# Pooled attention and a gated conv FFN on one core: the last output tile's halves in PSUM tiles of their own, and a new order of all queues

## The chip, the core and the metric

The kernel runs on one core of a Trainium2 chip. The metric is the device time in microseconds of one execution. TensorE (PE in the profile) does matmuls, VectorE (DVE) and ScalarE (ACT) elementwise work, GpSimd (POOL) and SyncE (SP) issue DMAs here, SyncE also the crossbar transposes.

## What is computed

With B = 8 batches, 8 heads, 576 rows and head size 64, in float32 outside and bfloat16 inside:

```python
k_p = k.reshape(B, H, Sp, 8, D).mean(axis=3)        # Sp = 72
v_p = v.reshape(B, H, Sp, 8, D).mean(axis=3)
attn = softmax(q @ k_p.T / sqrt(D))                  # 576 x 72 a head
x = (attn @ v_p), heads side by side                 # B, 576, 512
h = relu(x @ w_in)                                   # 512 -> 1024
gate = sigmoid(depthwise conv of h over 3 rows)
out = (h * gate) @ w_out                             # 1024 -> 512, float32
```

## The kernel before

All work is written down as some 1,075 small steps by a planner (`pl.add`), each with its engine, what it reads and writes, and the PSUM slot that it takes (`take`) or frees (`give`). In which order the steps are issued is not worked out in the kernel: it is the string `order` in `PARAMS`, a list of step numbers. Each engine and each DMA queue runs its steps in that order, waiting where a step needs another's result. The string also gives a matmul step its PSUM slot (`@A0` to `@A2` of twice 512 columns, `@B0` and `@B1` of 512), and `106A0/77` puts 106 units of filler matmuls (128 columns each, L231) ahead of step 77. The string `act` names the steps that ScalarE does out of those that VectorE could do as well. The table `alt` picks a variant of a step: for `x3.0`, 1 means a crossbar transpose issued by SyncE, none means four transposes on TensorE and a copy out of PSUM.

The names of the steps, with b the batch, t a tile of 128 rows, f one of 8 slices of the 1024 columns:

- `kT`, `kz`: the pooled k turned, and copied out of PSUM (L501, L507). `cw`: the conv weights in place (L361); `dw`: the identity scaled by one of them, for convs on TensorE (L407, L409).
- `qT`, `qTe`: q of batch 0 turned and copied (L567, L573); `qg`, `qD`: q of a later batch regrouped (L261) and turned by two crossbar transposes (L608).
- `sc`, `exp`: scores on TensorE and their exponential on ScalarE (L625 to L652). `av`, `rc`, `nm`: attention times v (L670, L674), reciprocal of the sums (L683), and the division (L687).
- `xt`, `xte` or `xD`: the tile of x turned, by TensorE and a copy (L701, L705) or by the crossbar (L710).
- `mm1`, `relu`: x times w_in (L732 for batch 0, L747) and relu (L738, L753).
- `cp`, `ca`, `conv`: the conv, as products and sums on ScalarE and VectorE (L769 to L781) or as matmuls (L800); `tanh`, `tg1`, `g`: the gate and its product with h, into `gT` (L788, L832, L838).
- `mm2`, `oe`, `st`: gT times w_out (L860), the copy out of PSUM (L883, or L873 for the last tile's halves), the store (L887, L878).

Two batches make a pair of nine output tiles; `mm2.3.8` is the last tile of the last pair. In the last pair, tiles 4 to 8 are summed in two pieces, slices 0 to 5 and then 6 and 7 (`cuts`). Of tile 8, the first piece is 512 columns wide, the second piece two halves of 256 columns in the same PSUM tile; each half is copied and stored by itself.

Of the kernel before, what the change touches and what calls it, by code (L numbers as in the profile page):

```python
# [56 lines left out]
    ),  # L57
    "act": (
# [7 lines left out]
    ),  # L66
    "alt": {"q1": 1, "v1": 1, "c0.5": 2, "c0.7": 2, "q2": 1, "c1.1": 1, "c1.3": 2, "q3": 1, "x3.0": 1, "x3.1": 1, "x3.2": 1, "x3.3": 1, "x3.4": 1, "c2.1": 1, "c2.5": 1, "q4": 1, "x4.0": 1, "x4.1": 1, "x4.2": 1, "x4.3": 1, "x4.4": 1, "c3.5": 1, "q5": 1, "x5.0": 1, "x5.1": 1, "x5.2": 1, "x5.3": 1, "x5.4": 1, "q6": 2, "x6.0": 1, "x6.1": 1, "x6.2": 1, "x6.3": 1, "x6.4": 1, "q7": 2, "x7.0": 1, "x7.1": 1, "x7.2": 1, "x7.3": 1, "x7.4": 1},
    "nq": 2,
    "nr": 1,
    "nx": 4,  # L70
# [72 lines left out]
def kernel(  # L143
# [10 lines left out]
    nc = tc.nc  # L154
# [3 lines left out]
    P = 128  # L158
# [809 lines left out]
```

## Time and profile before

| | us |
|---|---|
| median of 3 runs | 198.35 |
| lowest, highest | 197.63, 200.87 |
| the profiled execution | 196.67 |
| its span, first to last instruction | 195.0 |
| TensorE, VectorE, ScalarE, GpSimd busy | 186.5, 166.1, 167.0, 46.7 |
| TensorE clock granted | 1.00 all through |

The profiled execution is one of its own and a little faster than the three timed ones; its time is its span and 1.67 us around it. In the rows, `x4` is a count, and `<-` behind an idle time names what ended it. Two engines' rows that overlap in time ran beside each other. Matmuls overlap by a pipeline, so for them the distance of two starts tells the cost, not the length of one row.

### The profile page before, as it was taken

What the parts mean: (1) busy time and instruction counts of PE and PEld (TensorE: products, weight loads), DVE (VectorE), ACT (ScalarE), POOL (GpSimd) and SP (SyncE); (2) the same over time, 40 slices, a digit from 0 to 9 for tenths busy, and PEclk for the clock granted to TensorE, in tenths of its full rate; (3) what the DMA queues carried; (4) which work ended last, traced back from release to release, by engine and by line L of the source; (5) the groups of instructions that cost most, each with busy time, mean ns of one, the idle gap of its engine ahead of it and who ended that gap; (6) DMA issues with size and microseconds to landing.
All of it is one profiled execution on the core that took longest, in us unless ns stands there. A gap on an engine that the chain in (4) does not pass through costs nothing.

```text
span 195.0 us, 4515 instructions
## 1 busy us (share of the span) xinstructions
PE 186.5 (96%) x1730; PEld 124.3 (64%) x1746; DVE 166.1 (85%) x388; ACT 167.0 (86%) x301; POOL 46.7 (24%) x85
## 2 busy tenths in 40 slices
PE   7997999989999999999999999999999999999992
PEld 2465977665788878667667766685666566654441
DVE  3757789998589999999999899999999898999620
ACT  2088999955379999999999999999999999999931
POOL 8993354272055004363035000000000000000000
PEclk9999999999999999999999999999999999999999
DMA  5999999999939999999789999394003464105444
GB/s 193 210 163 202 203 203 208 203 206 204 152 50 172 203 205 157 195 96 201 152 135 180 200 296 140 89 186 118 14 0 95 151 196 170 54 0 217 170 156 161
DMA packets 40746, 30.72 MB, mean 158 GB/s; under 512 B 18556, under 2 KB 35668, under 8 KB 40724
## 3 DMA queue, kind: packets, MB, share of 16 engines
q0 software_dynamic: 17920, 15.67, 52.0%
q1 hardware_dynamic: 22804, 14.76, 30.2%
q8 instruction: 13, 0.21, 0.4%
q14 instruction: 9, 0.07, 0.1%
HBM read 32.52 MB, written 9.44 MB: 215 GB/s over the span
## 4 chain that ended last, share of the span: by engine, by line
PE 56%; ACT 17%; DVE 15%; DMA 8%; issue 2%; ACTq 0%; DVEq 0%
PE psfB L860 23%; PE psfA L747 17%; DMA q_b<-in_q_dram 5%; PE psfA L670 3%; ACT tg L788 3%; DMA osb<-in_k_dram 3%; ACT hT L753 3%; DVE gT L838 2%; DVE cv L776 2%; PE psfA L860 2%; DVE cv L781 2%; ACT cv L769 2%; DVE tg L832 2%; PE psfA L800 2%; PE psfA L674 2%
## 5 line engine op out<-in xcount | busy, mean ns | idle before, releaser
L860 PE MATMUL psfB<-w_out,gT 128*128 128x512 bf16 x260 | 62.2, 377 | 1.1 <-issue 0.3
L747 PE MATMUL psfA<-xT,w_in 128*128 128x288 bf16 x448 | 60.6, 286 | 0.0
L747 PEld LDWEIGHTS <-w_in 128*128 128x128 bf16 x448 | 43.3, 98 | 12.7 <-issue 0.2
L860 PEld LDWEIGHTS <-gT 128*128 128x128 bf16 x290 | 27.7, 98 | 30.4 <-issue 1.6
L788 ACT ACTIVATE tg<-cv,cs 128x576 bf16<-128x576 bf16 x54 | 42.2, 830 | 0.4 <-DVE cv L781 0.3
L753 ACT ACTIVATE hT<-psfA 128x576 bf16<-128x576 f32 x56 | 37.5, 692 | 4.8 <-PE psfA L747 4.5
L769 ACT ACTIVATE cv<-hT,cr 128x576 bf16<-128x576 bf16 x38 | 29.9, 830 | 0.0
L687 DVE TENSOR_TENSOR xx<-psfA,rr 128x512 bf16<-128x512 f32 x40 | 26.9, 687 | 0.7
L771 DVE TENSOR_SCALAR cv<-hT,cr 128x576 bf16<-128x576 bf16 x70 | 24.0, 369 | 1.1 <-ACT hT L738 0.7
L838 DVE TENSOR_TENSOR gT<-tg,hT 128x1152 bf16<-128x1152 bf16 x32 | 23.9, 754 | 0.4
L883 ACT COPY osb<-psfB 128x512 f32<-128x512 f32 x33 | 20.5, 643 | 4.2 <-PE psfB L860 3.0
L652 ACT ACTIVATE attnT<-psfA 128x576 bf16<-128x576 f32 x35 | 21.9, 664 | 0.5 <-PE psfA L644 0.3
L781 DVE TENSOR_TENSOR cv<-cv 128x1152 bf16<-128x1152 bf16 (+1 forms) x29 | 20.4, 710 | 1.1 <-ACT cv L769 0.5
L776 DVE TENSOR_TENSOR cv<-cv,hT 128x1152 bf16<-128x1152 bf16 (+1 forms) x29 | 20.5, 708 | 0.3 <-ACT cv L769 0.2
L295 POOL DMA_DIRECT2D v_b<-in_v_dram x32 | 16.3, 518 | 14.8 <-DVE vs L533 7.0
L670 PE MATMUL psfA<-vblk,attnT 128*128 128x130 bf16 x160 | 15.6, 221 | 1.3 <-ACT attnT L633 0.9
L832 DVE TENSOR_SCALAR tg<-tg 128x1152 bf16<-128x1152 bf16 x32 | 14.3, 454 | 1.6 <-ACT tg L788 1.5
L670 PEld LDWEIGHTS <-attnT 128*128 128x128 bf16 x160 | 11.8, 98 | 4.2 <-ACT attnT L633 1.3
L683 DVE RECIPROCAL rr<-psfA 128x8 f32<-128x8 f32 x40 | 7.3, 194 | 5.8 <-PE psfA L674 5.7
L231 PE MATMUL pswA<-zero 128*128 128x512 bf16 (+1 forms) x43 | 10.3, 385 | 1.1 <-DVE zero L333 1.1
L674 PE MATMUL psfA<-vblk,attnT 128*128 128x130 bf16 x80 | 11.2, 221 | 0.0
L644 PE MATMUL psfA<-qT,kz 128*128 128x288 bf16 x56 | 10.2, 286 | 0.1
(107 smaller groups left out, 220.4 us busy)
## 6 DMA issues: line engine op xcount, KB each, us to landing
out_dram<-osb SPq DMA_DIRECT2D x14, 512.0 KB, 3.7
q_b<-in_q_dram POOLq DMA_DIRECT2D x7, 576.0 KB, 9.4
k_b<-in_k_dram POOLq DMA_DIRECT2D x7, 512.0 KB, 10.0
v_b<-in_v_dram POOLq DMA_DIRECT2D x7, 512.0 KB, 8.4
out_dram<-osb SPq DMA_DIRECT2D x7, 256.0 KB, 2.2
osb<-in_k_dram SPq DMA_DIRECT2D x1, 1024.0 KB, 5.2
w_in<-in_moe_w_in_dram POOLq DMA_DIRECT2D x2, 512.0 KB, 10.1
w_out<-in_moe_w_out_dram POOLq DMA_DIRECT2D x2, 512.0 KB, 11.4
```

What stands on the lines that cost most here:

```text
L652: nc.scalar.activation(out=at(m)[:, t, :].rearrange("p (r i j) -> p r i j", i=2, j=3), in_=slot(key)[:, :, 0:HC].rearrange("p i (j r) -> p ...
L670: nc.tensor.matmul(out=a[:, g, c * w:(c + 2) * w], lhsT=attnT[m][:, S * s + u0:S * s + u0 + P], rhs=vblk[m][:, 2 * s:2 * s + 2, :].rearran ...
L687: nc.vector.tensor_tensor(out=xx[i3].rearrange("p (g h e) -> p g h e", g=2, h=4), in0=av_view()[:, :, :, 0:D], in1=rr[i3].rearrange("p (g ...
L747: nc.tensor.matmul(out=t[:, i, 0:HC], lhsT=w_in[:, c, f * P:(f + 1) * P], rhs=xT[m][:, c, i * HC:(i + 1) * HC], start=(c == 0), stop=(c == ...
L753: nc.scalar.activation(out=hT[m][:, f, 2:S + 2].rearrange("p (i x) -> p i x", i=2), in_=slot(key)[:, :, 0:HC], func=ACT.Relu)
L769: nc.scalar.activation(out=cv[y][:, kk // 2, z, :], in_=src, func=ACT.Copy, scale=sc)
L771: nc.vector.tensor_scalar(out=cv[y][:, kk // 2, z, :], in0=src, scalar1=sc, scalar2=None, op0=OP.mult)
L776: nc.vector.tensor_tensor(out=cv[y][:, 0, 0:n, :], in0=cv[y][:, 0, 0:n, :], in1=H4[:, f:f + n, 2:S + 2], op=OP.add)
L781: nc.vector.tensor_tensor(out=cv[y][:, 0, 0:n, :], in0=cv[y][:, 0, 0:n, :], in1=cv[y][:, 1, 0:n, :], op=OP.add)
L788: nc.scalar.activation(out=tg[i3][:, z, :], in_=cv[y][:, 0, z, :], func=ACT.Tanh if half else ACT.Sigmoid, scale=cs[:, f + z:f + z + 1] if ...
L838: nc.vector.tensor_tensor(out=o_, in0=tg[i3], in1=hT[b % 2][:, f:f + 2, 2:S + 2], op=OP.mult)
L860: nc.tensor.matmul(out=a[:, 0, j0:j1], lhsT=g[:, c, t * P:(t + 1) * P], rhs=w_out[:, c, j0:j1], start=(c == 0), stop=(c == n_fb - 1), skip ...
```

## The change

Three things change. First, each half of the last tile is a matmul group of its own over all eight slices, in a PSUM tile of its own, and each copy frees its own tile:

```diff
-                parts = [(0, 512)] if not final or c1 < n_fb else [(0, 256), (256, 512)]
+                parts = [(0, 256), (256, 512)] if final else [(0, 512)]
                 for y, (j0, j1) in enumerate(parts):
+                    key = (kind, pair, t, y) if final else (kind, pair, t)
+                    ky = ok + (y,) if final else ok
...
-                            nc.tensor.matmul(out=a[:, 0, j0:j1], lhsT=g[:, c, t * P:(t + 1) * P],
-                                             rhs=w_out[:, c, j0:j1], start=(c == 0), stop=(c == n_fb - 1), skip_group_check=final)
+                            nc.tensor.matmul(out=a[:, 0, 0:j1 - j0], lhsT=g[:, c, t * P:(t + 1) * P],
+                                             rhs=w_out[:, c, j0:j1], start=(c == 0), stop=(c == n_fb - 1))
...
                 for y in range(2):
+                    key = (kind, pair, t, y)
...
-                        copy_on(e)(out=osb[i3][:, 0, y * 256:(y + 1) * 256], in_=slot(key)[:, 0, y * 256:(y + 1) * 256])
+                        copy_on(e)(out=osb[i3][:, 0, y * 256:(y + 1) * 256], in_=slot(key)[:, 0, 0:256])
...
-                                reads=[ok + (y,)], writes=[("osb", i3, y)], give=key if y else None, after=oi)
+                                reads=[ok + (y,)], writes=[("osb", i3, y)], give=key, after=oi)
```

Second, `alt` loses `"x3.0": 1`, so that one piece of x is turned by TensorE. Third, the strings `order` and `act` are others: nearly every step moves on its engine, 71 steps change between ScalarE and VectorE, and the fillers are 180 units where they were 163 (106 of them ahead of the first `kT` in both). One line of the old and new string:

```diff
-        "15 52 0 41 4 44 16 53 47 18 49 60 50 57 61 46 56 58 73 55 3 17 74 59 75 54 76 5 43 1 106A0/77@B0 48 6@B1 86 78 7 51 28 19 29 "
+        "15 52 0 41 4 47 18 53 49 19 48 61 50 60 57 3 59 5 16 73 56 54 74 58 55 75 76 65 106A0/77@B0 6@B1 84@A0 7 36 21 78 86 17 85 62 42 "
```

Lines behind L854 stand three to five lines later in the changed kernel (L860 is L863, L873 is L878, L887 is L892).

ScalarE at the start, before and then changed. `dw` is the scaled identity, `kz` and `qT` the turned k and q of batch 0, `attnT` the exponentials; the words in brackets name the engine whose count a row waits for.

```order
L507 ACT_TABLE_LOAD [waits DVE_49]
L507 COPY kz_85<-psbB 64x4x72 [waits PE_49]
L407 ACTIVATE dw_114<-ident,cw 128x128 [waits DVE_49,Pool_49]
L407 ACTIVATE dw_115<-ident,cw 128x128
L341 COPY wrm<-wrm 128x1
L507 COPY kz_85<-psbB 64x4x72
L573 COPY qT_87<-psbB 128x12x64 [waits PE_49]
L573 COPY qT_87<-psbA 128x12x64 [waits PE_49]
L573 COPY qT_87<-psbB 128x24x32 [waits PE_49]
L633 ACTIVATE attnT_89<-psfB 128x384 [waits PE_49]
```

```order
L407 ACT_TABLE_LOAD [waits DVE_49]
L407 ACTIVATE dw_117<-ident,cw 128x128 [waits Pool_49]
L573 COPY qT_87<-psbA 128x24x32 [waits PE_49]
L573 COPY qT_87<-psbB 128x12x64 [waits PE_49]
L507 COPY kz_85<-psbB 64x4x72 [waits DVE_49]
L573 COPY qT_87<-psbA 128x12x64 [waits PE_49]
L633 ACTIVATE attnT_89<-psfB 128x384 [waits PE_49] x2
L633 ACTIVATE attnT_89<-psfA 128x384 [waits PE_49]
L407 ACTIVATE dw_116<-ident,cw 128x128
L633 ACTIVATE attnT_89<-psfB 128x384 [waits PE_49]
```

The table load is put ahead of ScalarE's first instruction and takes over its wait for VectorE: before, that was for the zeroing of kz, VectorE's second instruction; now it is for cw, its twelfth. One of the two kz copies has gone to VectorE, and the other stands between the qT copies.

VectorE around the second regrouping copy of q for batch 7 (`q_80<-q_b_79`), before and then changed. `rr` and `xx` are the reciprocal and the division of batch 6's attention tiles, `tg` and `gT` batch 3's gate, `cv` batch 4's conv.

```order
L447 TENSOR_TENSOR k_b_75<-k_b_75 128x5x128
L838 TENSOR_TENSOR gT_110<-tg_106,hT_102 128x2x576
L838 TENSOR_TENSOR gT_110<-tg_108,hT_102 128x2x576
L683 RECIPROCAL rr_94<-psfA 128x8
L683 RECIPROCAL rr_93<-psfA 128x8
L261 COPY q_80<-q_b_79 96x6x256
L771 TENSOR_SCALAR cv_104<-hT_101,cr 128x576
L687 TENSOR_TENSOR xx_97<-psfA,rr_93 128x512
```

```order
L687 TENSOR_TENSOR xx_98<-psfA,rr_94 128x512
L776 TENSOR_TENSOR cv_105<-cv_105,hT_101 128x1152
L683 RECIPROCAL rr_91<-psfA 128x8
L771 TENSOR_SCALAR cv_103<-hT_101,cr 128x576
L687 TENSOR_TENSOR xx_95<-psfA,rr_91 128x512
L261 COPY q_80<-q_b_79 96x6x256
L683 RECIPROCAL rr_92<-psfA 128x8
```

The copy stood ahead of the division of batch 6's first tile; now it stands behind that of its third. SyncE's two crossbar transposes for the scores of batch 7 follow it.

ScalarE at the end, the copies of the last output tiles, before and then changed (with the tiles' numbers).

```order
L883 COPY osb_111<-psfB_2896 128x512
L883 COPY osb_111<-psfB_2905 128x512
L883 COPY osb_111<-psfA_2918 128x512
L873 COPY osb_111<-psfB_2933 128x256 x2
L963 UNCONDITIONAL_BRANCH
```

```order
L888 COPY osb_111<-psfB_2907 128x512
L888 COPY osb_111<-psfA_2924 128x512
L878 COPY osb_111<-psfB_2936 128x256
L878 COPY osb_111<-psfB_2945 128x256
L968 UNCONDITIONAL_BRANCH
```

Both halves were read from one PSUM tile; now each is read from its own. On TensorE the first half's eight matmuls of 256 columns come first and the second half's eight after them, as the last work of that engine.

More of the change, by code (lines that the diff above doesn't have):

```diff
@@ L16 @@
     "order": (
[40 rows of a table removed]
[40 rows of a table added]
     ),
     "act": (
[7 rows of a table removed]
[7 rows of a table added]
     ),
-    "alt": {"q1": 1, "v1": 1, "c0.5": 2, "c0.7": 2, "q2": 1, "c1.1": 1, "c1.3": 2, "q3": 1, "x3.0": 1, "x3.1": 1, "x3.2": 1, "x3.3": 1, "x3.4": 1, "c2.1": 1, "c2.5": 1, "q4": 1, "x4.0": 1, "x4.1": 1, "x4.2": 1, "x4.3": 1, "x4.4": 1, "c3.5": 1, "q5": 1, "x5.0": 1, "x5.1": 1, "x5.2": 1, "x5.3": 1, "x5.4": 1, "q6": 2, "x6.0": 1, "x6.1": 1, "x6.2": 1, "x6.3": 1, "x6.4": 1, "q7": 2, "x7.0": 1, "x7.1": 1, "x7.2": 1, "x7.3": 1, "x7.4": 1},
+    "alt": {"q1": 1, "v1": 1, "c0.5": 2, "c0.7": 2, "q2": 1, "c1.1": 1, "c1.3": 2, "q3": 1, "x3.1": 1, "x3.2": 1, "x3.3": 1, "x3.4": 1, "c2.1": 1, "c2.5": 1, "q4": 1, "x4.0": 1, "x4.1": 1, "x4.2": 1, "x4.3": 1, "x4.4": 1, "c3.5": 1, "q5": 1, "x5.0": 1, "x5.1": 1, "x5.2": 1, "x5.3": 1, "x5.4": 1, "q6": 2, "x6.0": 1, "x6.1": 1, "x6.2": 1, "x6.3": 1, "x6.4": 1, "q7": 2, "x7.0": 1, "x7.1": 1, "x7.2": 1, "x7.3": 1, "x7.4": 1},
     "nq": 2,
@@ L859, in fn @@
                         for c in range(c0, c1):
-                            nc.tensor.matmul(out=a[:, 0, j0:j1], lhsT=g[:, c, t * P:(t + 1) * P],
-                                             rhs=w_out[:, c, j0:j1], start=(c == 0), stop=(c == n_fb - 1), skip_group_check=final)
-                    i = pl.add(f"mm2.{pair}.{t}.{c0}" + (f".{y}" if len(parts) > 1 else ""), "PE", (0.2165 * (j1 - j0) / 512 + 0.002) * (c1 - c0), fn,
+                            nc.tensor.matmul(out=a[:, 0, 0:j1 - j0], lhsT=g[:, c, t * P:(t + 1) * P],
+                                             rhs=w_out[:, c, j0:j1], start=(c == 0), stop=(c == n_fb - 1))
+                    i = pl.add(f"mm2.{pair}.{t}.{c0}" + (f".{y}" if final else ""), "PE", (0.2165 * (j1 - j0) / 512 + 0.002) * (c1 - c0), fn,
                                reads=[("gT", pair % 2, c, z) for c in range(c0, c1) for z in halves] + [("wo", 0), ("wo", 1)]
-                               + ([ok] if c0 else []),
-                               writes=[ok + (y,)] if len(parts) > 1 else [ok], take=key,
+                               + ([ky] if c0 else []),
+                               writes=[ky], take=key,
                                after=last_o[0] if not c0 else None)
```

92 rows, old and new, of the table PARAMS are left out of this document.

## The prediction

> **What bounds the kernel now.** I read the page's head first, then a table by stages, then the chain of waits backward from the end.
>
> ```profile
> span 195.0 us, 4515 instructions
> PE 186.5 (96%) x1730; PEld 124.3 (64%) x1746; DVE 166.1 (85%) x388; ACT 167.0 (86%) x301; POOL 46.7 (24%) x85
> ```
>
> ```profile
> core 0: us, PE busy (x) PEld busy (x) DVE busy (x) ACT busy (x) POOL busy (x), PEclk, DMA share, GB/s
> 15.00:30.00 15.00, 13.94 (x190) 11.42 (x191) 11.47 (x39) 14.08 (x38) 6.96 (x12) 1.00 1.25 203
> 30.00:42.70 12.70, 11.84 (x159) 8.89 (x159) 12.47 (x28) 10.79 (x23) 5.75 (x10) 1.00 1.24 205
> 42.70:75.00 32.30, 32.17 (x413) 24.06 (x415) 27.99 (x66) 24.16 (x43) 7.75 (x12) 1.00 1.09 169
> 75.00:125.00 50.00, 49.35 (x398) 34.01 (x402) 48.23 (x112) 49.19 (x84) 12.69 (x22) 1.00 1.00 168
> 125.00:165.00 40.00, 39.67 (x289) 25.86 (x293) 38.32 (x85) 39.68 (x67) 0.00 (x0) 1.00 0.44 118
> 165.00:191.40 26.40, 26.24 (x139) 13.43 (x139) 19.41 (x39) 22.17 (x38) 0.00 (x0) 1.00 0.31 121
> ```
>
> The reader is to see that from 42.7 to 191.4 us TensorE idles 0.13 + 0.65 + 0.33 + 0.16 = 1.27 us in 148.7. Busy could hide waits, so I looked at how fast it streams, in the chain of waits.
>
> ```profile
> 164.34 3.92 PE psfA L747 x32
> 173.67 6.20 PE psfB L860 x28
> 191.35 0.03 ACTq L873
> 191.42 0.37 ACT osb L873
> 191.79 0.27 ACTq L963
> ```
>
> 32 matmuls of 288 columns take 0.1225 us each and 28 of 512 columns 0.221 us, back to back. So from 42.7 us **TensorE's own work is the bound**: a new order there gains at most the 1.27 us, while each wait that it makes on TensorE is paid in full. VectorE and ScalarE are nearly as full (48.23 and 49.19 of 50 us in the third stage), so such waits are easily made. From 30.0 to 42.7 us VectorE is the full one (12.47 of 12.70), from 15 to 30 us ScalarE (14.08 of 15). After 191.4 us comes the tail.
>
> **The change part by part.** The sum is made against the profiled execution: 196.67 us, its span of 195.0 and 1.67 around it. The median of the runs shown is 198.35, 1.68 above that, and I add 1.68 at the end.
>
> *The tail.* Here are the last rows of ScalarE and SyncE on the timeline, and what the two stores' line says of landing.
>
> ```profile
> 191.42 0.65 ACT L873 COPY osb<-psfB 128x256 f32<-128x256 f32 x2 [1.07 <-PE psfB L860]
> 191.82 0.81 SPq L878 DMA_DIRECT2D out_dram<-osb  x2
> DMA to landing us min/median/max: 1.7/1.7/1.7
> ```
>
> Both copies start only after the last matmul, the second 0.28 after the first (0.65 less 0.37); the second store is issued at 191.82 + 0.81 - 0.38 = 192.25 and lands 1.7 us later, in the last us of the span. In the changed kernel the first half is complete 8 matmuls of 256 columns (half of 0.221, so 0.88 us) before the end; its copy (0.37) and store issue (0.33) lie beside those matmuls. The second half's copy then starts where the first one's did, and its store at 191.82 instead of 192.25: **-0.43 us**. On TensorE, six 512-column matmuls become twelve of 256, the same columns; I take 0 for it. Bounds: 0 if the store before it still holds up the queue, -0.65 if both copies went. For TensorE nothing is late behind it: it is its last work.
>
> *The transposed piece x3.0.* It leaves SyncE's crossbar transposes for TensorE.
>
> ```profile
> 42.23 0.39 PE L701 MATMUL psbB<-ident,xx 128*128 128x128 bf16 x4
> 42.45 0.22 PE L231 MATMUL pswB<-zero 128*128 128x128 bf16 x1
> L710 SPq DMA_TRANSPOSE xT<-xx x25: 1171/1230/2393, 72.3 to 156.6; - x25
> ```
>
> Four transposes take 42.45 - 42.23 = **+0.22 us** of TensorE, which is full there. The SyncE issue that goes (1.23 us) was not on the chain: I give no gain for it. The new copy out of PSUM goes to ScalarE.
>
> ```profile
> L771 DVE TENSOR_SCALAR cv<-hT,cr 128x576 bf16<-128x576 bf16 x70 | 24.0, 369 | 1.1 <-ACT hT L738 0.7 <-ACT tg L788 0.5
> L705 DVE COPY xT<-psbB 128x512 bf16<-128x512 bf16 x4 | 1.7, 415 | 0.3 <-PE psbB L701 0.3
> ```
>
> Between ScalarE and VectorE, by the order, 23 conv products leave ScalarE and 18 come; one kz copy and one output copy more leave than come; five copies of xT more come, x3.0's among them. VectorE gets five products at 24.0/70 = 0.34 us and the kz and output copies, and loses four xT copies at 0.42: about 1 us more, an estimate. This costs nothing as long as TensorE has work queued, and is kept in the upper bound below.
>
> *The start.* ScalarE and its partners before the first real work:
>
> ```profile
> 1.39 1.28 ACT L507 ACT_TABLE_LOAD   x1 [1.39 <-DVE kz L414]
> 9.42 0.39 ACT L507 COPY kz<-psbB 64x288 bf16<-64x288 bf16 x1 [6.74 <-PE psbB L501]
> 9.91 0.69 ACT L407 ACTIVATE dw<-ident,cw 128x128 bf16<-128x128 bf16 x2
> 11.55 0.80 ACT L573 COPY qT<-psbB 128x768 bf16<-128x768 bf16 x1 [0.46 <-PE psbB L567]
> 12.25 0.80 ACT L573 COPY qT<-psbA 128x768 bf16<-128x768 bf16 x1
> 13.65 0.50 ACT L633 ACTIVATE attnT<-psfB 128x384 bf16<-128x384 f32 x1
> 9.63 0.18 DVE L361 TENSOR_SCALAR cw<-psfB 128x24 f32<-128x24 f32 x1
> 16.23 0.40 PE L670 MATMUL psfA<-vblk,attnT 128*128 128x130 bf16 x4 [0.94 <-ACT attnT L633]
> ```
>
> Before, the table load sat at 1.39, hidden in ScalarE's idle 9 us. In the new order its first instruction is a scaling of the identity by cw, and the table load in front of it waits for VectorE up to cw, which ends at 9.81. Load 9.9 to 11.2; scaling, about 0.3; then from 11.5 three qT copies at 0.70 apart and one kz copy (0.4) in between end at about 14.1 (the last takes 0.8). The fill of 35 in front of the first score matmul ends there too: the qT transposes end about 12.25 and 35 x 0.0533 (a 512-column filler takes 0.213) is 1.87. So the first score starts near 14.15, the first exp near 14.55 against 13.65, and the first attention-times-v matmul near 14.55 + (16.23 - 13.65) = 17.1: **0.9 us late**.
>
> It does not stay. The first output product, at 42.72, waits for the last gate product, and for that VectorE is the bound:
>
> ```profile
> 23.49 0.82 DVE L443 TENSOR_TENSOR k_b<-k_b 128x1280 bf16<-128x1280 bf16 x1
> 26.45 0.70 DVE L771 TENSOR_SCALAR cv<-hT,cr 128x576 bf16<-128x576 bf16 x1 [0.67 <-ACT hT L738]
> 41.74 0.75 DVE L838 TENSOR_TENSOR gT<-tg,hT 128x1152 bf16<-128x1152 bf16 x1
> 42.72 2.53 PE L860 MATMUL psfB<-w_out,gT 128*128 128x512 bf16 x11
> ```
>
> From the row at 23.49 to the one at 41.74 both orders hold 45 VectorE instructions, and differ in six small ones on each side. With the lag of 0.9 the row at 23.49 would still start near 23.5, because in the new order the constants that stood ahead of it come elsewhere. The conv product at 26.45 had waited 0.67 for ScalarE; its slice came out of relu as first and seventh; the slice now taken first comes as second and fourth, so I give 0.2 of the 0.67 back: **-0.2 us** at 42.72. Bounds: -0.67, and +0.9 if VectorE cannot make up the lag. The fills after 16 us shrink from 29 units to 22, which is in this.
>
> A rule of the Trainium skill speaks against this part: the page "ScalarE: Activation LUTs", section "What ACT_TABLE_LOAD costs", gives a table load 1283 ns and a drain of about 1380 ns with it. The load agrees with the 1.28 us row; no drain shows behind it here, since ScalarE had nothing to do until 9.42. By that rule the start would be another 1.38 us later.
>
> *The last head's transpose, q of batch 7.* VectorE's regrouping copy now stands behind the row at 129.28 instead of at 122.44.
>
> ```profile
> 122.44 0.51 DVE L261 COPY q<-q_b 96x1536 bf16<-96x1536 bf16 x1
> 129.28 0.69 DVE L687 TENSOR_TENSOR xx<-psfA,rr 128x512 bf16<-128x512 f32 x1
> 125.13 3.01 SPq L608 DMA_TRANSPOSE qT<-q  x2
> DMA to landing us min/median/max: 3.5/3.8/4.6
> 133.17 0.65 PE L644 MATMUL psfA<-qT,kz 128*128 128x288 bf16 x4
> ```
>
> The two crossbar transposes start 3.01/2 = 1.5 apart, and the last lands up to 4.6 after its start: 6.1 from the first issue. The scores that need them stood at 133.17; by the order one output product (8 x 0.217 = 1.73) and x3.0 now stand ahead, so TensorE comes there at 135.1. VectorE reaches the copy between 128.3 (four conv instructions, 1.9 us, have gone behind it, others in front) and 129.97; it ends at 128.9 to 130.5 and the landing is at 135.0 to 136.6. TensorE waits 0 to 1.5, and every matmul behind it with it. I take **+0.2**, near the lower end, as the 1.9 us that left weigh more than what came.
>
> *All other places.* Some hundred instructions change places on full engines. The trace of before shows what that can give back, 1.27 us, and what it can cost only by its nearest rows: VectorE's extra 1 us, and single waits like the 0.94 at 16.23. I take 0, bounds -1.3 and +2.
>
> Sum: -0.43 + 0.22 - 0.2 + 0.2 + 0 = -0.2. So 196.5 us for a profiled execution and 196.5 + 1.68, about **198.1 us**, for a median. A measurement of this kernel can tell about 2%, some 4 us, from no change.
>
> **The rivals.** *The table load comes through.* If VectorE makes up nothing of the 0.9, the sum ends at +0.9 instead of -0.2 there: 199.2 us, slower than before. For it: the row at 41.74 shows VectorE full up to the end of that stage, so it has no slack to catch up with. Against: the lag ends before VectorE's full stretch starts at 26.45. It decides from the point where the first relu results come later than VectorE's k sums are done.
>
> *ScalarE is not free right behind its table load.* In the rows of before nothing stands on it from 2.67 to 9.42, so they do not exclude it. One more stretch of the load's own length, 1.28, on top of the lag gives 200.5 us. Against: nothing in the rows shows such a stretch. The page named above has this drain, and with its 1.38 it would be 200.6.
>
> *A landing in the middle.* The q transposes land at the late end, 136.6, and another such wait joins it at a piece of xT: +1.5 and +1 over the forecast's +0.2, 200.4 us. More than 2% slower would need almost 4 us of waits on TensorE; three times the worst that I find.
>
> *The waits go.* The 1.27 us of idle after 42.7 vanish, as do the 0.86 before (12.70 - 11.84): 198.1 - 2.1 = 196.0 us. For it: they are scattered, so a finer order can take them. Against: full engines make new ones. Faster by 2% would need a further 2 us, only to be had from the start, which I see later, not earlier.
>
> *The tail does not shorten.* If the halves' copies stay together, for instance since the stores queue behind the one before, 0.43 is lost: 198.5 us.
>
> **How the numbers follow.** Forecast, within a us of 198.1: 0.56, of which the rival of the tail has 0.06. The lag comes through: 0.10. ScalarE busy behind the load: 0.05. A landing: 0.09. Waits go: 0.20. From these, slower by over 2% is 0.04 (parts of the second to fourth), faster by over 2% 0.04 (the far end of the last), and 0.92 lies within. The range reaches from waits gone (196.0, less 0.3, part of the start's lower bound) to the landing with the tail's 0.43 lost as well (200.8): 195.7 to 200.8. Single runs shown lie between 197.63 and 200.87, which asks for no less.
>
> **What would show it.** Right: ScalarE's table load at about 9.9 us; the first output product within 0.7 of 42.7; one L701 group of four more; the copy of the first half about 0.8 us ahead of the last matmul's end, and about 3.2 us from that end to the end of the span (195.0 - 191.35 = 3.65 before). Wrong: TensorE idle in front of the scores of batch 7, or in any stage after 42.7 by over 1 us more than before; or a first output product before 42.0 or after 43.5.

## The result and the profile after

| | before | changed |
|---|---|---|
| median, us | 198.23 | 197.19 |
| lowest, highest | 197.57, 200.87 | 196.05, 198.67 |
| the profiled execution | 196.67 | 197.41 |
| its span | 195.0 | 194.8 |

20 timed runs each. The ratio is 0.9942, with a 95% interval of 0.9922 to 0.9963: faster by 0.6%, 0.7 to 1.5 us. The ratios here and below leave out executions that took over 1.5% longer than the fastest of their kernel, and need not equal the quotient of two medians. Forecast were 198.1 us, in a range of 195.7 to 200.8. The two profiled executions differ by only 0.2 us of span, because the one of before was a lucky one: its 196.67 lies below all 20 timed runs of before. That 0.2 is also what the sum had for a profiled execution is luck: the changed kernel's load of k landed 1.2 us later (7.26 against 6.05), which no term of the sum has.

The same parts of the page and the same stretches as before, now of the changed kernel:

```profile
span 194.8 us, 4531 instructions
PE 186.7 (96%) x1741; PEld 125.4 (64%) x1758; DVE 165.9 (85%) x391; ACT 165.2 (85%) x299; POOL 45.7 (23%) x85
```

```profile
core 0: us, PE busy (x) PEld busy (x) DVE busy (x) ACT busy (x) POOL busy (x), PEclk, DMA share, GB/s
30.00:42.70 12.70, 12.40 (x158) 8.86 (x156) 12.18 (x27) 12.26 (x26) 5.47 (x13) 1.00 1.04 158
42.70:75.00 32.30, 32.20 (x423) 24.07 (x423) 27.25 (x67) 23.89 (x43) 11.58 (x18) 1.00 1.22 196
75.00:125.00 50.00, 49.74 (x404) 34.69 (x406) 48.95 (x113) 48.89 (x84) 11.25 (x19) 1.00 0.88 156
125.00:165.00 40.00, 39.49 (x288) 25.43 (x291) 39.27 (x88) 39.30 (x66) 0.00 (x0) 1.00 0.47 126
165.00:191.40 26.40, 26.24 (x149) 14.59 (x150) 19.80 (x40) 22.35 (x38) 0.00 (x0) 1.00 0.32 122
```

Behind 42.7 us TensorE idles 0.10 + 0.26 + 0.51 + 0.16 = 1.03 us, where it was 1.27. The middle is what it was. The tail, on the timeline:

```profile
189.78 1.91 PE L863 MATMUL psfB<-w_out,gT 128*128 128x256 bf16 x16
...
190.90 0.37 ACT L878 COPY osb<-psfB 128x256 f32<-128x256 f32 x1 [0.17 <-PE psfB L863]
191.29 1.16 SPq L883 DMA_DIRECT2D out_dram<-osb  x2
191.72 0.37 ACT L878 COPY osb<-psfB 128x256 f32<-128x256 f32 x1 [0.46 <-PE psfB L863]
```

The last matmul ends at 189.78 + 1.91 = 191.69. The first half's copy starts 0.79 ahead of that. From that end to the end of the span there are 3.16 us, where there were 3.62 (with the spans unrounded, 194.84 and 194.97).

That leaves half of the gain unexplained, and neither of the two profiles shows it. The next section finds most of it in executions of before that are not like the profiled one: by their mean clock, TensorE runs at half clock for some 3.4 us in most of them, and two profiles with before's start show where, between 16.5 and 20.3 us.

### The profile page after: what moved, and what is told of

It reads as the page before. It is cut to its first block, busy times and chain, and to the rows that moved or that the text cites. A ratio compares the mean times of both kernels' runs of the same rounds, so it can differ in the third digit from the quotient of the medians.

```text
span 194.8 us, 4531 instructions
## 1 busy us (share of the span) xinstructions
PE 186.7 (96%) x1741; PEld 125.4 (64%) x1758; DVE 165.9 (85%) x391; ACT 165.2 (85%) x299; POOL 45.7 (23%) x85
## 4 chain that ended last, share of the span: by engine, by line
PE 56%; DVE 20%; ACT 16%; DMA 3%; issue 2%; DVEq 0%
PE psfB L863 20%; PE psfA L747 16%; ACT tg L788 4%; DVE xx L687 3%; PE psfA L670 3%; DMA osb<-in_k_dram 3%; DVE cv L771 3%; DVE cv L776 3%; ACT attnT L652 3%; DVE gT L838 2%; DVE cv L781 2%; PE psfA L863 2%; PE psfA L644 2%; ACT hT L738 2%; PE psfA L800 2%
## 5 line engine op out<-in xcount | busy, mean ns | idle before, releaser
L863 PE MATMUL psfB<-w_out,gT 128*128 128x512 bf16 (+1 forms) x266 | 62.1, 373 | 0.7
L863 PEld LDWEIGHTS <-gT 128*128 128x128 bf16 x296 | 28.5, 98 | 28.1 <-DVE gT L838 0.3
L788 ACT ACTIVATE tg<-cv,cs 128x576 bf16<-128x576 bf16 x54 | 40.9, 779 | 0.8 <-DVE cv L781 0.8
L753 ACT ACTIVATE hT<-psfA 128x576 bf16<-128x576 f32 x56 | 36.0, 658 | 2.9 <-PE psfA L747 2.6
L771 DVE TENSOR_SCALAR cv<-hT,cr 128x576 bf16<-128x576 bf16 x75 | 25.7, 367 | 1.1 <-ACT hT L738 0.8
L769 ACT ACTIVATE cv<-hT,cr 128x576 bf16<-128x576 bf16 x33 | 24.9, 776 | 0.1
L888 ACT COPY osb<-psfB 128x512 f32<-128x512 f32 x32 | 18.5, 588 | 5.5 <-PE psfB L863 5.5
L231 PE MATMUL pswA<-zero 128*128 128x512 bf16 (+1 forms) x42 | 10.9, 420 | 1.4 <-DVE zero L333 1.1
```

The source lines that it names most:

```text
L753: nc.scalar.activation(out=hT[m][:, f, 2:S + 2].rearrange("p (i x) -> p i x", i=2), in_=slot(key)[:, :, 0:HC], func=ACT.Relu)
L769: nc.scalar.activation(out=cv[y][:, kk // 2, z, :], in_=src, func=ACT.Copy, scale=sc)
L771: nc.vector.tensor_scalar(out=cv[y][:, kk // 2, z, :], in0=src, scalar1=sc, scalar2=None, op0=OP.mult)
L788: nc.scalar.activation(out=tg[i3][:, z, :], in_=cv[y][:, 0, z, :], func=ACT.Tanh if half else ACT.Sigmoid, scale=cs[:, f + z:f + z + 1] if ...
L863: nc.tensor.matmul(out=a[:, 0, 0:j1 - j0], lhsT=g[:, c, t * P:(t + 1) * P], rhs=w_out[:, c, j0:j1], start=(c == 0), stop=(c == n_fb - 1))
```

## The experiments

All are timed beside before on the same chip, in three sets: the first four rows, the next four, the last four. The columns from the fourth on: in how many executions the mean granted clock of the whole run was at least 0.995; from each kernel's profile the start of the first output product (A), the time from there to the end of TensorE's last matmul (B), and from there to the end of the span (C). Before had 198.38, 198.31 and 198.05 us in the three sets, and full clock in 27 of 93 executions; its two profiles show A 42.72 and 44.33, B 148.62 and 148.35, C 3.6. The changed kernel had full clock in 19 of 20; A 43.28, B 148.41, C 3.2.

| | median, us | ratio to before, 95% | full clock | A | B | C |
|---|---|---|---|---|---|---|
| tail_only | 198.52 | 0.9988, 0.9963 to 1.0014 | 2 of 12 | 44.52 | 148.31 | 3.1 |
| order_only | 197.47 | 0.9958, 0.9933 to 0.9982 | 12 of 12 | 45.10 | 148.36 | 3.7 |
| x3_crossbar | 197.52 | 0.9958, 0.9932 to 0.9983 | 10 of 12 | 42.73 | 148.90 | 4.8 |
| before_again | 198.02 | one run | 0 of 1 | 44.33 | 148.35 | 3.6 |
| before_start | 197.80 | 0.9998, 0.9968 to 1.0029 | 1 of 12 | 44.09 | 148.51 | 3.2 |
| after_start | 196.92 | 0.9966, 0.9929 to 1.0003 | 12 of 12 | 43.58 | 148.39 | 3.6 |
| const_early | 197.06 | 0.9970, 0.9938 to 1.0002 | 12 of 12 | 42.50 | 148.69 | 3.2 |
| early_table_short_fill | 197.51 | 0.9957, 0.9924 to 0.9989 | 6 of 12 | 42.99 | 149.12 | 3.2 |
| before_filled | 197.80 | 0.9998, 0.9972 to 1.0024 | 12 of 12 | 43.61 | 148.31 | 3.6 |
| tail_filled | 197.11 | 0.9952, 0.9929 to 0.9976 | 11 of 12 | 42.96 | 149.03 | 3.1 |
| after_thin | 198.90 | 1.0036, 1.0013 to 1.0058 | 0 of 12 | 45.12 | 148.69 | 3.2 |
| all_in | 196.63 | 0.9896, 0.9851 to 0.9940 | 4 of 6 | 41.93 | 148.41 | 3.2 |

The executions of one kernel scatter by 1.7 to 5.2 us, so a ratio is worth about ±0.25% at best. In the second set the ratio and the medians differ: by the medians of all executions, before_start is at 0.997 of before and after_start at 0.993. B and C are of one profile each; B ranges over 0.8 us in the 14 profiles; C is steadier, but for x3_crossbar.

### The parts of the change

*tail_only*: the kernel before, with the halves of the last tile as changed.

```diff
-mm2.3.8.0  mm2.3.8.6.0  mm2.3.8.6.1      (one PSUM tile)
+mm2.3.8.0.0  mm2.3.8.6.0                 (the first half's own tile)
+mm2.3.8.0.1  mm2.3.8.6.1                 (the second half's own tile)
```

> The order of before, with the last tile's halves in PSUM tiles of their own (first half's eight matmuls, then the second half's) and nothing else. Theory of the prediction: the tail alone gives 0.43 to 0.55 us, so about 197.7 against 198.2 for before, and in the profile 3.1 us from the last matmul's end to the end of the span where before had 3.65. Rival (the gain is all in the new order): no change in the time, and the same 3.65.

*order_only*: the changed order and `alt`, with the three old steps of the last tile.

> The changed kernel's order and x3.0 on TensorE, with the last tile as before (one PSUM tile, the first piece 512 wide). Theory of the prediction: what remains of the gain of 1.05 us without the tail, about 0.5, so 197.7. Rival (the gain is all in the new order): 197.2, as the changed kernel. Rival (the order gives nothing): 198.2.

*x3_crossbar*: the changed kernel with that piece back on the crossbar.

```diff
+"x3.0": 1
-xt.3.0  xte.3.0
+xD.3.0
```

> The changed kernel with x3.0 turned by the crossbar again, issued by SyncE where TensorE did it. Theory of the prediction: TensorE is full, its four transposes cost 0.22 us, so 0.2 faster than the changed kernel. Rival (the crossbar's landing would hold up the first product of batch 3, or SyncE's queue): the same or slower by up to a us.

*before_again*: a second profile of the kernel before.

> The kernel before, unchanged, for a second trace of its start. The load of k landed at 6.05 us in the trace of before and at 7.26 in that of the changed kernel. If that is the scatter of one load, it lands anywhere between 6 and 7.5 here, and the first output product moves with it: 42.7 for 6.05, about 43.9 for 7.26. If the changed kernel's own order of loads delays it, it lands near 6.05 again and the first output product is at 42.7.

The tail is seen in column C: 3.62 to 3.70 us in the five profiles with the old tail, and 3.09 to 3.17 in eight of the nine with the new one. In the profile of tail_only the last matmul ends at 190.91 + 1.91 = 192.82, 3.1 us ahead of the end of its span of 195.9:

```profile
190.91 1.91 PE L863 MATMUL psfB<-w_out,gT 128*128 128x256 bf16 x16
```

x3_crossbar is the ninth, with 4.84:

```profile
192.92 0.65 ACT L878 COPY osb<-psfB 128x256 f32<-128x256 f32 x2 [2.29 <-DMA out_dram<-osb]
```

Both copies waited there until an earlier store had landed (issued at 188.43, landed at 192.82), and then ran one behind the other. So the halves overlap only where the stores ahead of them land in time. The time of tail_only alone, -0.1%, is too uncertain to show 0.5 us. Two runs below of the same set, before_filled and tail_filled, differ by the tail alone and have medians 0.69 us apart, each uncertain by some tenths. The order brings 0.4% by itself, and column B says that it does not come from behind 43 us: 148.62 and 148.35 in the two profiles of before, 148.36 in order_only. A saving of 0.22 with x3.0 on the crossbar does not show in B (148.90), but is smaller than the range of B.

### Where the order's gain sits

*before_start* has before's order up to the first output product and the changed one behind it; *after_start* the reverse, with the old tail and x3.0 as before.

```diff
 before_start:
-order of the changed kernel up to mm2.0.0.0
+order of before up to mm2.0.0.0
 after_start:
-order of before up to mm2.0.0.0
+order of the changed kernel up to mm2.0.0.0
```

> The changed kernel, with before's order up to the first output product and the changed order behind it (tail and x3.0 as changed). Theory that the new start carries the order's gain: behind the second batch's k fold the old start took 18.6 to 19.2 us to the first output product and the new one 18.2 to 18.9, so about 0.4 us of the changed kernel's gain is lost: 197.6, ratio to before 0.997. Rival, the gain is in the order behind 43 us: 197.2, ratio 0.994. By both, the stretch from the first output product to TensorE's last matmul stays at 148.3 to 148.9 us.

> The kernel before, with the changed order up to the first output product only; old tail, old order behind it, x3.0 by the crossbar. Theory that the new start carries the order's gain: 198.2 - 0.4 = 197.8, ratio 0.998. Rival, the gain is in the order behind 43 us: 198.2, ratio 1.000. A lag of 0.9 that came through, as the prediction's rival had it, would give 199.1, ratio 1.005.

The start carries it: with the old start almost nothing is left of the gain by the ratio, and 0.3% by the medians, in spite of the new tail; the new start alone brings 0.3% by the ratio, barely to be told from nothing, and 0.7% by the medians. But the 0.4 us that I had worked out from the k fold on is not the main thing. The mean clock is: the old start has full clock in 1 of 12 executions and 2 of 12 (tail_only), the new one in all 12 and all 12 (order_only). What is left beside the clock is small: against those executions of before on the same chip that had full clock, order_only is 0.36 us faster (197.47 against 197.83, the median of seven) and after_start 0.25 (196.92 against 197.17, of nine).

Before_again, one of the 0.991 kind, shows where the clock falls. The stretches are the ones that the trace's clock rows give: in every profile the clock changes only at whole multiples of 3.413 us from its first rise.

```profile
core 0: us, PE busy (x) PEld busy (x) DVE busy (x) ACT busy (x) POOL busy (x), PEclk, DMA share, GB/s
13.44:16.85 3.41, 2.20 (x20) 0.93 (x15) 2.47 (x8) 3.41 (x11) 3.15 (x5) 1.00 1.22 188
16.85:20.27 3.42, 3.42 (x32) 3.00 (x32) 2.20 (x6) 1.88 (x7) 0.53 (x2) 0.50 1.22 196
20.27:23.68 3.41, 3.35 (x77) 2.85 (x75) 2.49 (x9) 2.90 (x6) 1.25 (x3) 1.00 1.24 205
```

In the window from 13.44 TensorE is busy 2.20 of 3.41 us, with small q transposes and scores on 32 rows among it and 0.94 of idle at its end. In the next window it gets half the clock, 32 matmuls instead of 77. The execution of before that the prediction read had the same instructions with its windows elsewhere:

```profile
11.03:14.45 3.42, 3.35 (x108) 2.41 (x109) 2.19 (x8) 2.96 (x7) 3.42 (x6) 1.00 1.11 150
14.45:17.86 3.41, 2.27 (x28) 1.48 (x27) 2.00 (x7) 3.08 (x12) 2.06 (x4) 1.00 1.26 204
16.85:20.27 3.42, 3.36 (x73) 2.99 (x73) 3.28 (x10) 2.89 (x8) 0.78 (x2) 1.00 1.21 198
```

There the thin stretch is cut in two, and the clock stays. The busy times of these two windows, 2.20 with a fall and 2.27 without, are too close to tell what decides. Two other profiles tell more, before_start (first two rows) and order_only (last two):

```profile
13.09:16.50 3.41, 2.37 (x31) 1.05 (x25) 1.97 (x7) 3.41 (x10) 2.47 (x4) 1.00 1.16 166
16.50:19.92 3.42, 3.25 (x31) 2.87 (x32) 2.03 (x6) 1.89 (x8) 0.51 (x1) 0.50 1.20 195
26.07:29.48 3.41, 1.82 (x22) 1.48 (x20) 2.61 (x10) 1.69 (x7) 1.10 (x2) 1.00 1.26 203
29.48:32.90 3.42, 3.25 (x26) 2.21 (x25) 3.32 (x12) 3.15 (x9) 1.73 (x4) 1.00 1.25 194
```

The clock falls behind 2.37 us of work with no gap above 0.78 in the window, and stays behind 1.82 us with a gap of 1.59. So neither the busy time nor the longest gap decides alone. Another count does separate them: each matmul's columns, times the share of the 128 weight columns that it uses, added up and taken as a share of what fits the window at 512 columns in 0.213 us. The windows ahead of a fall hold 0.28 to 0.36 in the four profiles that have one (the hundredths depend on how a matmul across an edge is counted), and every other window of the 14 profiles up to 40 us at full clock holds 0.39 or more. By this count a window is called thin below; it is a reading of these traces, not a rule that was tried. Where the windows lie differs from run to run: their first rise came between 3.9 and 6.6 us. So the same program pays the stretch in some executions and not in others, and the kernel before, by the mean clock, pays it in 66 of 93 (58 show about one stretch, 8 more than that).

The Trainium skill, page "TensorE: Matmul & The Clock Gate", part on the clock gate, "What's actually happening", has such a window: 3413 ns, running free of the kernel's start, with half the clock after an idle one. The length and the free run agree with these rows. That it takes an idle window does not: here it fell behind one in which TensorE was busy for 2.20 us, with no gap above 0.94.

What does the stretch cost? The 27 executions of before at full clock have a median of 197.33 us, the 58 with one stretch 198.29, the 8 with more 199.54. By set of runs the medians at full clock and below it are 197.83 and 198.53, 197.17 and 198.56, 197.95 and 198.15: 0.7, 1.4 and 0.2. That it goes along with the time is shown by this; that it causes it was the next question.

### VectorE's constants and the table load

*const_early* moves fifteen small VectorE steps to where VectorE idled.

```diff
 dw4.0
+dw3.1 dw5.1 cna cn0 dw3.2 cn1 cn2 cr2 dw2.1 cr0 cs dw3.0 dw4.1 zvt1 v81
 (each taken out of its place between nm.0.1 and ca0.0.2)
```

> The changed kernel, with fifteen small VectorE steps (scaled identities and conv constants, about 3.2 us together, which stand between 21 and 30 us) moved to where VectorE idles, 15.4 to 18.5 us, behind dw4.0 and ahead of the first reciprocal. Theory that VectorE sets the first output product: it comes 0.6 to 1.0 us earlier behind the same k fold, 196.4 in all, ratio to before 0.991. Rival, the loads' landings and the relu results behind them set it: no change against the changed kernel, 197.2, ratio 0.994.

*early_table_short_fill* issues ScalarE's table load first and shortens two fillers.

```diff
 zero
+wz aw
-17A1/qT.0.0.0   35A2/sc.0.1.0
+ 3A1/qT.0.0.0   20A2/sc.0.1.0
```

> The changed kernel, with two other small ScalarE steps issued first, so that the table load stands at about 1.4 us instead of 10.9, and with 14 units fewer of filler ahead of a q transpose and 15 fewer ahead of the first score. Theory that the landings and VectorE behind them absorb the lag of the first scores: first score about 1 us earlier, first output product and time unchanged, 197.2, ratio to before 0.994. Rival, the lag comes through to the end: 196.2 to 196.4, ratio 0.990.

const_early gives the changed kernel's time, not 0.8 less: its first output product comes at 42.50, but VectorE then waits for the load of the second batch's k, which had landed at 23.99, 0.09 ahead of the fold. early_table_short_fill has its first score at 13.63 instead of 15.25 and gains nothing either: its VectorE waits 0.35 us for the same load, and with fewer fillers the clock fell in half of its executions.

### The fillers and the clock

*before_filled* is before with filler in the gap; *tail_filled* has the new tail as well; *after_thin* is the changed kernel without two of its fillers.

```diff
 before_filled, tail_filled:
-av.0.0@A0
+16B1/av.0.0@A0
 after_thin:
-17A1/qT.0.0.0   35A2/sc.0.1.0
+qT.0.0.0   sc.0.1.0
```

> The kernel before, with one edit: 16 units of filler matmuls (0.85 us) ahead of the first attention-times-v matmul, where TensorE idled 0.94. Theory of the half-clock stretch: those executions of before whose mean clock is 0.991 have TensorE at half clock for 3.41 us near 16.5 to 20 us, behind a window of 3.41 us in which TensorE did little, and cost 0.8 to 1.0 us; with the gap filled the clock is 1.00 in nearly all executions, and the median falls to 197.4 to 197.7, ratio 0.996. Rival, the clock only goes along with late landings that cost the time anyway: the clock rises and the time stays, 198.3, ratio 1.000.

> The kernel before with the halves of the last tile in PSUM tiles of their own (as changed) and the same 16 units of filler; its order and x3.0 otherwise as before. If the tail and the half-clock stretch are the whole of the gain: 198.3 - 0.5 - 0.8 = 197.0, ratio 0.994, as the changed kernel. Rival, the new order brings something of its own elsewhere: 197.6 or more, ratio 0.997.

> The changed kernel without two of its fillers: the 17 units ahead of a q transpose and the 35 units (1.87 us) ahead of the first score. The first score comes up to 0.8 us earlier, as nothing is computed ahead of it but q and k. Theory of the half-clock stretch: the window in front holds too little TensorE work, the clock falls to half for 3.41 us in most executions (mean 0.991), and the time rises by 0.3 to 0.8 in spite of the earlier score: 197.5 to 198.0, ratio 0.997 to 0.999. Rival, fillers only delay: 196.8, ratio 0.992.

That thin windows make the clock fall is shown both ways: 16 units of filler bring before's order from 27 of 93 executions at full clock to 12 of 12, and taking 52 units out of the changed kernel brings it from 19 of 20 to none of 12. In after_thin the clock is half for three windows:

```profile
9.25:12.67 3.42, 2.26 (x104) 1.98 (x101) 1.49 (x7) 2.58 (x4) 2.13 (x4) 1.00 1.20 182
12.67:22.91 10.24, 7.37 (x52) 5.42 (x54) 5.38 (x18) 7.17 (x19) 2.76 (x7) 0.50 1.20 187
22.91:26.32 3.41, 3.23 (x79) 2.90 (x78) 2.69 (x11) 3.28 (x8) 0.89 (x2) 1.00 1.24 206
```

That this costs time is shown by after_thin too: 198.90 us, 1.7 above the changed kernel (on another chip) and 0.4% slower than before on the same chip, against an expected rise of 0.3 to 0.8, though its three windows are more than I had counted on. Its first score stands at 14.45 us, behind a q copy that it waits 2.94 us for. At the first attention-times-v matmul it is still 0.45 us ahead of the changed kernel's profile (17.52 against 17.97); from there VectorE takes 8.66 us to the second batch's k fold, against 6.41, with no wait for the load in either. So the loss falls in the stretch at half clock, 12.67 to 22.91 us.

before_filled, on the other hand, missed its 197.4 to 197.7: it has the clock and only 0.25 us of the gain by the medians, and by its ratio, 0.9998, none. A reason can be read in the start of the second batch's k fold and in what it waited for. In before_again the load was issued at 13.21 and took the 9.6 of the last row, so it landed at 22.8; the fold started at 25.48, as VectorE came late from the half-clock stretch:

```profile
25.48 0.81 DVE L443 TENSOR_TENSOR k_b<-k_b 128x1280 bf16<-128x1280 bf16 x1
```

```profile
L278 POOL DMA_DIRECT2D k_b<-in_k_dram x1: 807/807/807, 13.2 to 13.2; - x1
...
DMA to landing us min/median/max: 7.6/8.6/9.6
```

In tail_only, at full clock, VectorE was there in time and waited for the load instead, until 25.93:

```profile
25.93 0.83 DVE L443 TENSOR_TENSOR k_b<-k_b 128x1280 bf16<-128x1280 bf16 x1 [1.04 <-DMA k_b<-in_k_dram]
```

With the old start and the stretch VectorE comes to the fold at 25.2 to 25.5 (before_start, before_again), without the stretch by 23.5 (before). Counted from the first attention-times-v matmul that is 8.55 and 8.63 us against 7.26, so the stretch costs about 1.4 us here; the other 0.6 between 23.49 and 25.48 was there already, behind a first load of k that landed at 6.62 instead of 6.05. This load landed between 22.4 and 26.6 us in the 14 profiles. Where it is early the stretch is paid in full, where it is late, as in tail_only, a start without the stretch gains nothing by it. In before_filled another load held the start up, that of w_in:

```profile
21.32 0.40 PE L732 MATMUL psfA<-xT,w_in 128*128 128x128 bf16 x4 [0.47 <-DMA w_in<-in_moe_w_in_dram]
```

```profile
24.30 0.81 DVE L443 TENSOR_TENSOR k_b<-k_b 128x1280 bf16<-128x1280 bf16 x1
```

w_in landed at 21.28 there and at 19.72 in before. VectorE came to the fold at 24.30, after the landing of k at 24.10, 7.82 us behind the first attention-times-v matmul. The filler itself delayed nothing: that matmul stands 3.13 us behind the first score with it and without it. So how much a set of runs shows depends on its landings, 0.2 to 1.4 us above; that the third set's were later was not measured run by run, and stays open. The 0.25 of before_filled agrees with its own set, in which before's executions at full clock were ahead by only those 0.2.

tail_filled does what the whole change does, within the noise: 197.11, ratio 0.9952, with the old order, the old places of 71 steps and x3.0 on the crossbar. The new order as such was not needed for the gain.

### A version beyond both

*all_in* is the changed kernel with the table load first, fillers where TensorE really waits, and twelve constants ahead of the k fold.

```diff
 zero
+wz aw
-17A1/qT.0.0.0   35A2/sc.0.1.0   av.0.0
+ 3A1/qT.0.0.0   28A2/sc.0.1.0   18A1/av.0.0
 dw4.0
+cna cn0 dw3.2 cn1
 nm.0.4
+cn2 cr2 dw2.1 cr0 cs dw3.0 dw4.1 v81
```

> The changed kernel with the table load at about 1.4 us, 18 units of filler in the gap ahead of the first attention-times-v matmul and fewer ahead of the first score (28 and 3 instead of 35 and 17), and twelve small VectorE constants moved ahead of the second batch's k fold. Theory: clock 1.00 all through, first output product 0.5 to 1.0 earlier behind the same landings: 196.2 to 196.7, ratio to before 0.990. Rival, the landings of the loads hold it: 197.2, ratio 0.994.

```profile
span 193.5 us, 4531 instructions
```

```profile
24.01 0.82 DVE L443 TENSOR_TENSOR k_b<-k_b 128x1280 bf16<-128x1280 bf16 x1 [1.03 <-DMA k_b<-in_k_dram]
```

196.63 us over six executions, 1.0% faster than before (0.6% to 1.5%) by the ratio; by the medians of all, 0.7%, as one of the six took 199.70 us. VectorE now waits 1.03 us for the load, and from the fold to the first output product (41.93 by the table) there are 17.9 us, where the changed kernel has 18.9. That it beats the changed kernel is likely but not settled: they did not share a chip, and their intervals overlap.

## Why the prediction was right, and where it was not

**The bound** was right. From the first output product on, TensorE's own work sets the time: column B stays within 148.3 and 149.1 us in 14 profiles, with either order behind it.

**The tail**, -0.43, was right in its mechanism and its size: from 3.62 us to 3.16. The rival that the halves' copies stay together is out for eight of nine profiles; in x3_crossbar it came true, behind a late store.

**x3.0**, +0.22, is in the work: the weight loads of these transposes went from 60 to 64.

```profile
L701 PEld LDWEIGHTS <-xx 128*128 128x128 bf16 x64 | 4.3, 98 | 1.4 <-issue 0.6 <-DVE xx L687 0.3
```

But x3_crossbar, without them, was not faster (B 148.90 in place of 148.41, 197.52 us), so the term is not confirmed as a cost; B of one profile cannot exclude it either.

**The start**, -0.2: the table load came late, as worked out, and the lag did not come through.

```profile
10.88 1.28 ACT L407 ACT_TABLE_LOAD   x1 [10.88 <-DVE cw L361]
12.17 0.40 ACT L407 ACTIVATE dw<-ident,cw 128x128 bf16<-128x128 bf16 x1
...
15.61 0.87 ACT L633 ACTIVATE attnT<-psfB 128x384 bf16<-128x384 f32 x2 [0.41 <-PE psfB L625]
```

The load of k landed 1.2 us later in this execution, and so all of it stands about a microsecond behind the forecast's 9.9. The next instruction starts 0.01 us behind the load's end (10.88 + 1.28), so the rival of a ScalarE that is busy behind it is out, and the drain of about 1380 ns, which the Trainium skill gives on its page "ScalarE: Activation LUTs", section "What ACT_TABLE_LOAD costs", does not show. The first output product came at 43.28, within the 0.7 of 42.7:

```profile
43.28 1.03 PE L863 MATMUL psfB<-w_out,gT 128*128 128x512 bf16 x3
```

The first attention-times-v matmul was 1.74 us later than before (17.97 against 16.23), the k fold 0.88 later (24.37 against 23.49), and the first output product 0.56. What makes up for the lag was named only in part. That less stands ahead of the fold in the new order was foreseen, and it holds in this profile, where VectorE came to the fold 0.70 after the load had landed. In the six other profiles with the new start and full clock, or with one stretch of half clock, VectorE waited 0.35 to 2.61 us for that load, so there the landing absorbs the lag, and also the earlier scores of early_table_short_fill. And VectorE is not the one full engine ahead of the first output product any more: from 30.0 to 42.7 us TensorE is busy for 12.40, ScalarE for 12.26 and VectorE for 12.18 of 12.70.

**q of batch 7**, +0.2, was 0. VectorE's copy stood at 128.50, inside the bounds, the two crossbar transposes were issued from 129.07, and the second landed at 134.91. The scores start at 135.64 with no wait in front, and would have had none at the forecast's 135.1 either:

```profile
129.07 3.04 SPq L608 DMA_TRANSPOSE qT<-q  x2
```

```profile
133.91 1.89 PE L863 MATMUL psfB<-w_out,gT 128*128 128x512 bf16 x8
135.64 0.65 PE L644 MATMUL psfA<-qT,kz 128*128 128x288 bf16 x4
```

The forecast's 1.5 us between the two transposes was read too long: half of the row's 3.01 counts the second issue's own length with it, and the starts were 1.37 apart in before and 1.33 here.

**All other places**, 0, was right: 1.03 us of idle in place of 1.27. The extra microsecond of VectorE's work, an estimate, did not show: it was busy for 165.9 us in place of 166.1.

**The step that failed** is the last one, "196.5 + 1.68". It took the distance between the profiled execution and the median of before as a constant of the machine. It was not: the profiled execution was of the kind in which the clock stays full, 27 in 93, and the median one has the half-clock stretch. The new start takes the stretch away in 19 of 20 executions, so its median stands 0.2 below its own profiled execution, not 1.68 above. No term of the sum has this stretch: that 197.19 lies within a microsecond of 198.1 is the width of the forecast, which had -0.2 us against before where -1.04 was measured. A second miss went the other way and hid part of the first: the profiled execution took 197.41 instead of 196.5, with 2.6 us around its span instead of 1.67. The size of the gain fits: 0.5 of the tail, and about 0.65 of the stretch (the mean of all 93 executions of before is 198.25, that of the 27 at full clock 197.60), against 1.04 measured. That the split is exactly this is not shown, since before_filled brought less. The rival of vanishing waits, 196.0, had the right sign, but the waits behind 42.7 hardly changed.

## What to carry to other kernels

Ask whether the profiled execution is a typical one before adding a constant to it: its time against the timed runs, and the mean clock of several executions, tell. A matmul engine that is kept busy with fillers should have them where it really waits, so that no window of 3.41 us is thin; the 0.85 us of filler that stood in a wait of 0.94 delayed nothing. Work moved off a full engine gains only up to the next transfer that lands there.

## What was not expected of the hardware

The granted clock falls to half for one window of 3.41 us behind a window in which TensorE was busy for 2.20 to 2.37 us of 3.41, with no gap above 0.94 (before_again, before_start). By the mean clock this meets 66 of 93 executions of the same program, while a window with 1.82 us of work and a gap of 1.59 passed without a fall (order_only). The load of the second batch's k, issued at 12.0 to 13.2 us in the 14 profiles, landed between 22.4 and 26.6 us. In the seven profiles in which VectorE waited for it, the first output product came 18.0 to 18.7 us behind the landing; in the others VectorE came later than the load.
